# A long convolution in front of a gated MLP: cosine phases made on TensorE for twelve groups, and a fourth of the transform's copies on VectorE

## The chip, the cores and the metric

The kernel runs on one core of a Trainium2 chip. The metric is the time of one execution in microseconds (us) on the device, the median of several runs. In the profile PE is TensorE, DVE is VectorE, ACT is ScalarE, POOL is GpSimd and SP is SyncE, which issues DMAs.

## The reference

```python
# x: 2048 positions x 576 channels; 128 complex poles for each channel
dt = exp(log_dt);  logdA = dt * (A_re + 1j*A_im);  dB = dt * B
P = exp(logdA[:, :, None] * arange(2048))             # 576 x 128 x 2048
K = einsum("dn,dnl,dn->dl", C, P, dB).real            # the convolution's kernel
h = layernorm(x) * (1 + ca) + sa
x = x + ga * (causal_conv(h, K) + h * Dskip)          # through FFTs of length 4096
h = layernorm(x) * (1 + cb) + sb
z = gelu(h @ w_in)                                    # 576 -> 4608
z1, z2 = z[..., :2304], layernorm(z[..., 2304:])
x = x + gb * ((z1 * (w_sp @ z2 + b_sp)) @ w_out)      # w_sp: 2048 x 2048
```

`sa` to `gb` are six rows of `silu(c) @ w_mod`.

## The kernel before

**Two parts.** `ssm` is the convolution; the class `Mlp` is the rest. The change lies in `ssm`, in about the first 155 us. There every operation is issued in the order in which the program writes it (the wrapper at lines 223 and 224 pins it, which is why the profile gives line 224 for nearly everything). That order is a written table, `ORDER` (from line 55): each word is one step of a unit, such as `t5` for the next step of `t_unit(5)`, and `Steps.go` runs them one by one. Each engine takes its own instructions in this order, and an instruction that waits holds all behind it on its engine.

**Poles.** `poles` computes the logarithms and angles of the poles, first for chunk 0 (steps `O0`), then for chunks 1 to 3 (steps `P0`); each number is split into three bfloat16 parts (`pt`) and stored to DRAM (`pa_d`, `pb_d`). `poles_load` (line 392) reads a chunk back into `lb`, `lc` and `la`: two halves at partitions 0 to 47 and 64 to 111. The partitions 32 to 63 of `lb` are first set to zero by POOL, since one matmul reads all 112.

**Groups.** There are 36 groups `g` of 16 channels. `e_unit` makes the magnitudes: matmuls of `lb` with the table `sel` into a double PSUM bank, then exponentials on ACT into `et`. `t_unit` (line 578) makes the phases. For a group in `ROUNDED` (among them all of 0 to 13) PE fills one `ps` tile of 128x1024 with twelve matmuls: it adds a large constant, adds the phase in turns (`phases` with `lc` and `la`), takes the constant away again, so that only the rounded number of turns is left, and subtracts the phase. What stands in PSUM is then minus the phase's fraction of a turn. I call these twelve matmuls a fill. DVE writes its absolute value to half of an `ft` tile (for the cosine); ACT writes the sine to the other half, straight from PSUM, and then the cosine from the absolute value, as a sine with a bias of a quarter turn. The `ps` tiles are two (`ps2`, shared with `e_unit`), the `ft` tiles three, the single-bank `pk` tiles four (`ps1`); the table `PLAN` says which use takes which. `p_unit` (line 621) multiplies `ft` with `et` on DVE, `kg_unit` contracts the products over the poles on PE and `k1_unit` makes the first transform stage of the kernel.

**The input's transform.** `mod_unit` makes the rows of `silu(c) @ w_mod`: matmuls of `wm`, `k_a` or `k_b` with `ec`, a copy to `mpart` on ACT, a second matmul with ones, then `gar`, `cga` and `sga`. `ln_rows` scales rows of x with `cga` on DVE. `ln_half` (line 540, sixteen calls, steps `A0` to `A15`) transforms them: matmuls into four `pk` tiles, four copies of 128x288 from there to `st1o` on ACT, and a DMA issued by POOL. `st1o` has two buffers.

After that, groups, the products with the input's transform and the way back (`u_unit`, `z_unit`, `v_unit`, `y_unit`) go on until about 340 us, followed by the MLP.

Of the kernel before, what the change touches and what calls it, by code (L numbers as in the profile page):

```python
# [9 lines left out]
F32 = mybir.dt.float32  # L10
# [20 lines left out]
COPIED = set()  # L31
PLAN = {
    "et": "0123401232013423014021304123024104120",
    "ft": "012021201201021201202102101201012102",
# [7 lines left out]
    "ps": "01010010100101111010101001010101010101011001001110100101001011000101010101010101010101010101010101010101010101"  # L42
        "0101",
# [11 lines left out]
B0 O0 O0 O0 O0 B2 O0 O0 O0 O0 B7 O0 B1 O0 O0 O0 B6 O0 O0 O0 O0 O0 O0 x0 O0 O0 O0 O0 P0 S0 O0 S0 B3 O0 O0 i2 O0 O0 O0 P0 M2 O0 O0 S0 S0 B4 P0 S0 O0 Q0 P0 e1 S0 M2 e1 i1 e0  # L55
P0 P0 g0 e1 e0 P0 e0 e1 P0 t1 t2 i0 g1 O0 M2 e0 P0 M1 t1 t2 t1 P0 P0 t0 w3 P0 M1 t0 M2 t1 t0 t2 M1 M0 M1 M0 t0 e2 j1 R1 P0 p1 M3 t2 M0 p1 M3 R0 e2 R3 e6 p1 M0 B5 e2 M0 e6
M3 w4 k1 e4 e2 P0 M3 k1 O0 P0 e3 11 p0 e4 11 e6 M4 M0 e5 p0 P0 p0 e6 S1 S1 p2 M4 k0 M4 p2 11 R2 p2 e5 k0 e5 S1 M0 M3 M0 P0 k2 M4 e5 M0 P0 t5 k2 A0 e3 A0 S1 A0 A0 A0 w5 t5
S1 e3 P0 e3 A0 t3 S1 A1 t5 A1 A1 r2 A1 P0 t3 R4 A1 t7 A0 R5 A1 A2 A2 O0 P0 t3 t3 A2 A2 t4 P0 A1 A2 A2 A3 p3 A2 A3 t5 P0 r3 A3 A3 t4 t4 j2 M4 10 10 e4 A3 A3 A3 e4 12 p3 12
e7 p3 e7 P0 e7 R7 t7 10 R6 P0 p5 S2 12 k3 e8 e7 O0 k3 e8 A4 S2 A4 S2 A4 e8 S2 A4 A4 A4 e8 p5 P0 A5 t4 A5 A5 P0 A5 p5 A5 p4 A5 t7 a4 A4 A5 t6 A6 A6 A6 p4 A6 t6 A6 p4 A6 t8
A7 A7 P0 t7 A7 A7 O0 k4 A6 P0 S2 A7 13 t6 p7 A7 k4 t8 p7 R9 14 13 O0 k5 P0 P0 a5 t6 14 14 t8 p7 Q1 13 t8 M5 x3 k7 P0 e11 R8 A7 k5 M5 S3 k7 S3 A8 A8 e11 R11 e9 A8 e10 e11  # L60
P0 e9 e11 P0 p6 S3 S3 A8 P0 A8 R10 t10 A8 e10 A9 t10 A9 A9 A9 p8 p8 r6 e10 A9 A9 t9 e10 t10 A10 A8 P0 A10 A10 A10 A9 t11 p6 A10 A10 17 P0 t10 M5 p6 17 k6 M5 p8 t11 t9 17
k6 A11 A11 r7 S3 t11 t11 e12 A11 A11 Q2 15 R13 A11 A11 A10 p11 k8 t9 15 15 R12 A11 k8 A12 p11 A12 e12 A12 p11 A12 e14 A12 t14 A12 A13 e14 p10 A13 t14 A13 R15 e9 p10 A13
p10 A13 R14 A13 e9 t14 A12 e12 t12 e12 A14 A14 t9 A14 t15 A14 A14 t12 A13 t14 A14 t12 A15 A15 t14 O0 O0 A15 e16 k10 P0 A15 P0 A15 16 A15 P0 O0 p9 t12 k11 16 M5 p9 A14 A15
p9 C0 16 t14 18 c1 k10 f0 18 110 k11 18 110 e14 U2 110 U1 U0 t15 p12 111 t15 111 z2 111 t15 u2 t16 p12 u2 U5 p12 u0 e14 k9 c0 z2 z2 u0 k9 t16 k12 U4 p14 u1 19 U14 t16 U7
e16 k12 e15 19 t16 19 U23 e13 e15 e15 e16 u1 e15 c3 u7 e16 e13 p14 u4 u7 e13 u4 p14 c2 p15 z1 z1 e13 t13 U29 v2 u14 U6 t16 v2 p15 z4 U10 u14 t13 u6 t13 p15 t18 k15 z4 u6
u5 t16 k15 z1 p16 t18 p16 u29 e18 u5 U15 v1 z0 t13 u29 t18 e17 X1 t18 v1 U3 e18 115 115 u10 v1 v2 z0 u10 z0 X3 p16 e17 115 k14 k14 u3 b1 e17 e22 u3 p13 U12 e22 t17 e17
# [20 lines left out]
def consts():  # L87
# [64 lines left out]
    sel = np.zeros((112, 2368))  # L152
    sel[:48, :1024] = sel[64:, :1024] = half
# [7 lines left out]
    sel[:48, 1024:1280] = sel[64:, 1280:1536] = rge.reshape(48, 256)  # L161
# [75 lines left out]
def ssm(tc, I, x1_d, consts_s, dram, mod_d, mlp):  # L237
# [6 lines left out]
    with ExitStack() as ctx:  # L244
# [23 lines left out]
        sel = tb.tile([112, 2368], BF, name="sel", bufs=1)  # L268
# [132 lines left out]
        def rows(c0, w):  # L401
            return [sel[64 * h:64 * h + 48, c0:c0 + w] for h in range(2)]

        def halves(t, gi):
            return [t[64 * h:64 * h + 48, gi] for h in range(2)]
# [134 lines left out]
        def ln_half(k):  # L540
# [22 lines left out]
        def e_unit(g):  # L563
# [10 lines left out]
            T.matmul(pb, lb[:, gi], sel[:, 1024:1536], start=True, stop=True)  # L574
# [3 lines left out]
        def t_unit(g):  # L578
            c, gi = divmod(g, 9)
            pa = ps2()  # L580

            def phases(cols, start, stop):
                for k, (n, c0) in enumerate(zip(("lc", "la"), cols)):
                    for h, (l, r) in enumerate(zip(halves(lt[n, c], gi), rows(c0, 256))):
                        T.matmul(pa[:, h].rearrange("p (c k j) -> p k c j", c=8, k=2)[:, k], l, r, start=start, stop=stop, skip_group_check=True)

            def magics(c0, start):
                for h, (l, r) in enumerate(zip(rows(c0, 128), rows(2048, 64))):
                    T.matmul(pa[:, h].rearrange("p (c j) -> p c j", c=8), l, r[:, None, :].to_broadcast([48, 8, 64]), start=start, stop=False,
                             skip_group_check=True)  # L590
# [1877 lines left out]
```

## Time and profile before

| | |
|---|---|
| runs | 1691.24 to 1698.08 us, median 1694.87 of 3 |
| profiled execution | 1691.0 us, its span 1688.9 us |
| PE, DVE, ACT busy over the span | 96%, 77%, 52% |
| of the 20 us from 60 to 80: PE, DVE, ACT busy | 13.3, 19.3, 19.7 |
| from 80 to 100 | 16.3, 19.4, 18.3, granted clock 0.67 |
| from 120 to 140 | 15.4, 19.6, 19.4, granted clock 0.98 |
| from 220 to 240 | 20.0, 20.0, 19.6, granted clock 1.00 |

PE's busy time is modelled from pipelined matmuls, so a busy PE is not PE at its peak. The granted clock is the share of TensorE's full clock. In the rows of the timeline the columns are the start in us, the duration in us, the engine, the operation as output<-inputs, its shape, and in brackets the idle time of the engine just before it and what ended it. An engine begins an instruction before the one ahead has quite ended, so the step from start to start is shorter than the duration.

### The profile page before, as it was taken

Reading aid. Unit: us, or ns where it says so; the run is one execution under the profiler, and the core shown is the slowest. Engines: PE = TensorE matmul, PEld = TensorE weight load, DVE = VectorE, ACT = ScalarE, POOL = GpSimd, SP = SyncE. Lnnn points to the kernel's source line nnn. Section 1 sums busy time; section 2 is a strip of 40 time slices with the busy share of each in tenths; the row PEclk is TensorE's granted clock in tenths of the full one; section 3 lists DMA queues with packets and bytes.
Section 4 is the critical chain, followed back from the end, with each engine's and each line's share of the span. In section 5 each row is a group of like instructions: output and inputs, shape, how many; then the busy total and the mean of one; then the engine's idle time right before and its main releaser. Section 6 shows DMA issues by size and latency. Waiting matters only on the chain.

```text
span 1688.9 us, 39922 instructions
## 1 busy us (share of the span) xinstructions
PE 1615.6 (96%) x16868; PEld 1235.7 (73%) x16868; DVE 1298.4 (77%) x2241; ACT 873.8 (52%) x1307; POOL 209.7 (12%) x340
## 2 busy tenths in 40 slices
PE   3778999989999999999999999999999999999999
PEld 1344677755555557778878888888888888888887
DVE  7898999867989877988997776894443487787555
ACT  6889999675776664555444433342321133353221
POOL 3251111112222110000000000000111100111100
PEclk9978999999999999999999999999999999999999
DMA  9667645596888898776738887664667573777560
GB/s 231 170 215 229 203 140 176 171 317 208 280 287 243 251 261 297 242 270 234 249 118 302 282 292 257 219 218 166 232 213 243 189 221 121 275 281 252 189 241 29
DMA packets 186402, 380.61 MB, mean 225 GB/s; under 512 B 38464, under 2 KB 105792, under 8 KB 185456
## 3 DMA queue, kind: packets, MB, share of 16 engines
q1 hardware_dynamic: 145216, 182.10, 35.2%
q0 software_dynamic: 34528, 169.11, 30.1%
q10 hardware_dynamic: 6480, 26.86, 3.9%
q8 instruction: 132, 2.16, 0.5%
q14 instruction: 46, 0.38, 0.1%
HBM read 272.73 MB, written 105.29 MB: 224 GB/s over the span
## 4 chain that ended last, share of the span: by engine, by line
PE 77%; DVE 7%; DMA 3%; issue 2%; ACT 2%; SPq 0%; POOL 0%; ACTq 0%; DVEq 0%; POOLq 0%
PE ps L224 58%; PE pz L224 10%; PE pk_b L224 2%; PE pk_a L224 2%; DMA zset<-set_d 2%; PE pk_c L224 2%; PE pk_d L224 1%; DVE zset L224 1%; DVE gt L224 1%; DVE bsz L224 1%; PE ps_a L224 0%; PE ps_b L224 0%; DMA v_d<-v_a 0%; PE pt L224 0%; DMA uu_a<-in_x 0%
## 5 line engine op out<-in xcount | busy, mean ns | idle before, releaser
L224 PEld LDWEIGHTS <-zset 128*128 128x128 f16 x7182 | 702.2, 98 | 86.5 <-DMA zset<-set_d 2.0
L224 PE MATMUL ps<-wsp,zset 128*128 128x256 f16 x6048 | 666.8, 273 | 2.2 <-DMA zset<-set_d 1.1
L224 PE MATMUL pz<-wz,nt 128*128 128x512 f16 (+1 forms) x1120 | 220.8, 358 | 1.5 <-ACT nt L224 1.0
L224 ACT ACTIVATE z<-gt 128x1024 f16<-128x1024 f32 x56 | 59.0, 1054 | 250.4 <-DVE gt L224 250.4
L224 PEld LDWEIGHTS <-nt 128*128 128x128 f16 x1120 | 109.4, 98 | 107.1 <-ACT nt L224 1.5
L2164 POOL DMA_DIRECT2D zset<-set_d x96 | 50.8, 529 | 862.5 <-PE ps L224 619.7
L224 PE MATMUL ps<-wout,z 128*128 128x288 f16 x1092 | 138.4, 286 | 0.0
L224 DVE SCALAR_TENSOR_TENSOR gt<-ps,sc,bsp 128x512 f32<-128x512 f32 x36 | 27.0, 749 | 143.0 <-PE ps L224 141.3
L224 PEld LDWEIGHTS <-z 128*128 128x128 f16 x1176 | 115.1, 98 | 28.9
L224 DVE TENSOR_TENSOR raw<-raw 128x256 f32<-128x256 f32 (+3 forms) x238 | 126.8, 539 | 7.7 <-DMA raw<-z_d 3.5
L224 PE MATMUL ps<-n2o,zset 128*128 128x256 f16 x1134 | 128.2, 273 | 0.0
L224 DVE SCALAR_TENSOR_TENSOR gt<-ps,sc,gt 128x512 f32<-128x512 f32 (+1 forms) x180 | 122.2, 696 | 7.6
L224 ACT ACTIVATE zset<-raw 128x1792 f16<-128x1792 f32 x48 | 81.1, 1691 | 59.3 <-PE ps L224 21.6
L224 DVE TENSOR_TENSOR zset<-raw,zset 128x1792 f16<-128x1792 f32 x48 | 96.9, 2020 | 15.7 <-ACT zset L224 15.7
L224 DVE TENSOR_TENSOR z<-ps,z 128x512 f32<-128x512 f32 (+1 forms) x126 | 72.0, 599 | 32.3 <-ACT z L224 25.9
L224 ACT ACTIVATE z<-pz,sc 128x512 f32<-128x512 f32 (+1 forms) x96 | 51.9, 574 | 39.9 <-PE pz L224 32.7
L224 ACT ACTIVATE wsp<-raw,sc 128x1792 f16<-128x1792 f32 x25 | 44.5, 1783 | 46.2 <-DVE raw L224 40.2
L224 ACT ACTIVATE z<-z,sc 128x1024 f32<-128x1024 f32 x21 | 24.1, 1148 | 76.0 <-DVE z L224 72.3
L224 ACT ACTIVATE z1b<-gt 128x512 f16<-128x512 f32 (+1 forms) x22 | 17.7, 821 | 84.0 <-DVE gt L224 84.0
L224 PE MATMUL ps<-n2q,wf 128*128 128x512 f16 x252 | 55.7, 379 | 0.0
L224 DVE BATCH_NORM_STATS2 bsz<-z 128x6 f32<-128x384 f32 x96 | 48.4, 548 | 5.0 <-ACT z L224 4.4
L224 DVE SCALAR_TENSOR_TENSOR wsp<-raw,sc,wsp 128x1792 f16<-128x1792 f32 x25 | 52.0, 2078 | 0.3 <-ACT wsp L224 0.3
(793 smaller groups left out, 2772.0 us busy)
## 6 DMA issues: line engine op xcount, KB each, us to landing
zset<-set_d POOLq DMA_DIRECT2D x96, 896.0 KB, 5.2
raw<-z_d SPq DMA_DIRECT2D x48, 512.0 KB, 5.6
set_d<-zset ACTq DMA_DIRECT2D x24, 896.0 KB, 6.4
z_d<-z POOLq DMA_DIRECT2D x32, 576.0 KB, 8.2
zset<-wa_d POOLq DMA_DIRECT2D x18, 896.0 KB, 4.9
raw<-in_w_spT SPq DMA_DIRECT2D x25, 512.0 KB, 4.4
set_d<-zset SPq DMA_DIRECT2D x12, 896.0 KB, 5.8
wst<-in_w_in SPq DMA_DIRECT2D x8, 1024.0 KB, 9.3
```

The lines of the kernel that those rows point to most:

```text
L224: return self.tc.keep_in_program_order(f(*a, **k))
L2164: self.nc.gpsimd.dma_start(o, self.set_d[f, j - 1] if j else self.wa_d[f])
```

## The change

For the groups 0 to 11 (`TWICE`) PE makes a second fill into the other `ps` tile, a quarter turn on: `sel` has one more row for each half, which holds a quarter, and the partition behind each half of `lc` and `la` is set to one, so that the matmuls of `phases` take 49 rows instead of 48. Both sine and cosine are then a plain sine on ACT, straight from PSUM; the absolute value on DVE falls away. The steps of such a unit are still four. `lb`, `lc` and `la` become two fixed tiles each, and their constant parts are set once by DVE: the first tiles in `begin(0)`, the second in `begin(4)`; POOL's four memsets go. In `ln_half` the third of the four copies goes from ACT to DVE (`SHARED`). `ORDER` and the rings `ft` and `ps` of `PLAN` are written anew for the early part, up to the last `A` steps.

```diff
+TWICE = set(range(0, 12))
+SHARED = {2}
...
-P0 P0 g0 e1 e0 P0 e0 e1 P0 t1 t2 i0 g1 O0 M2 e0 P0 M1 t1 t2 t1 P0 P0 t0 w3 P0 M1 t0 M2 t1 t0 t2 M1 M0 M1 M0 t0 e2 j1 R1 P0 p1 M3 t2 M0 p1 M3 R0 e2 R3 e6 p1 M0 B5 e2 M0 e6
+e0 P0 P0 g0 e1 e0 P0 e0 e1 P0 t1 t1 i0 g1 O0 M2 e0 P0 M1 t1 P0 P0 w3 P0 M1 M2 t0 t1 t0 t0 t2 t0 t2 M1 M0 M1 M0 t2 e2 j1 R1 P0 t2 p1 M3 M0 p1 M3 R0 e2 R3 e6 p1 M0 B5 e2
...
-    sel = np.zeros((112, 2368))
+    sel = np.zeros((113, 2368))
...
+        sel[h + 48, :256] = sel[h + 48, 768:1024] = 0.25
+        sel[h + 48, 1536:2048] = -0.25
...
+        ltiles = {n: [tb.tile([112 if n == "lb" else 113, 9, 128], BF, name=n + i, bufs=1) for i in "ab"] for n in ("lb", "lc", "la")}
+
+        def fill(i):
+            for n, t in ltiles.items():
+                if n == "lb":
+                    V.memset(t[i][32:64], 0.0)
+                else:
+                    V.memset(t[i][32:64], 1.0)
+                    V.memset(t[i][96:113], 1.0)
...
-                t_ = tb.tile([112, 9, 128], BF, name=n)
-                if n == "lb":
-                    Q.memset(t_[32:64], 0.0)
+                t_ = ltiles[n][c % 2]
...
             for g, pm in enumerate(pms):
-                A.activation(o[:, g], pm[:, :HC], AF.Copy)
+                if g in SHARED:
+                    V.tensor_copy(o[:, g], pm[:, :HC])
+                else:
+                    A.activation(o[:, g], pm[:, :HC], AF.Copy)
...
+            def rounded(pa, r):
+                magics(pa, 2112, True)
+                phases(pa, (768, 0), False, False, r)
+                magics(pa, 2240, False)
+                phases(pa, (1536, 1792), False, True, r)
...
+            if g in TWICE:
+                rounded(pa, 48)
+                yield
+                pc = ps2()
+                rounded(pc, 49)
+                yield
+                ct, f = places()
+                A.activation(f, pa, AF.Sin, scale=-TWO_PI)
+                yield
+                A.activation(ct, pc, AF.Sin, scale=-TWO_PI)
+                return
...
             if n == 0:
+                fill(0)
                 p0 = poles(0, 1, G, ring(tb, [128, 1536], F32, "et", 5))
...
             elif n == 4:
+                fill(1)
                 S.dma_start(small, I["c_small"].rearrange("p (i c) -> p i c", i=7))
```

`places` takes the `ft` tile, as `t_unit` did before. `magics` and `phases` do what they did, with the tile and the number of rows as arguments. In the two rows of `ORDER`, between the first `M1` steps (the matmuls of `k_a`) and the third (the matmul with ones that `cga` waits for), there stand the PE steps of `t0` once before; now both PE steps of `t0` and both of `t2`, with ACT's steps of `t1` and `t0` among them.

On DVE, in the pole work for chunks 1 to 3, after layer norm's means (`nm`), the change puts the second set of memsets:

```order
58 L228 TENSOR_SCALAR nm<-nm 128x4
59 L228 MEMSET lbb 32x576
60 L228 MEMSET lcb 32x1152
61 L228 MEMSET lcb 17x1152
62 L228 MEMSET lab 32x1152
63 L228 MEMSET lab 17x1152
64 L228 TENSOR_SCALAR t_rnd<-t_n_A_im 128x432
```

Before, `nm` and `t_rnd` followed each other. A little further on, DVE before the change has the absolute values of the first three groups around the splitting of the poles (`t_tau` to `t_sq`), ahead of `cga`:

```order
80 L224 TENSOR_TENSOR t_n_B_im<-t_n_B_im,t_rnd 128x432
81 L224 TENSOR_SCALAR ft_a<-ps_a 128x1024
82 L224 TENSOR_SCALAR ft_b<-ps_b 128x1024
83 L224 TENSOR_SCALAR t_tau_223<-t_n_A_im 128x432
84 L224 TENSOR_SCALAR t_rnd<-t_tau_223 128x432
85 L224 TENSOR_TENSOR t_tau_223<-t_tau_223,t_rnd 128x432
86 L224 TENSOR_TENSOR t_sq_403<-t_n_A_re,pt 128x432
87 L224 TENSOR_TENSOR t_sq_405<-t_n_A_im,pt 128x432
88 L224 TENSOR_SCALAR ft_c<-ps_a 128x1024
89 L224 SCALAR_TENSOR_TENSOR cga<-pk_c,gar 128x288
```

In the change the rows 81, 82 and 88 are gone and the others stand in the same order. On ACT, at the same place, before the change:

```order
40 L224 ACTIVATE mpart<-pk_d 128x288
41 L224 ACTIVATE gar<-pk_a 128x288
42 L224 ACTIVATE gar<-pk_b 128x288
43 L224 ACTIVATE ft_a<-ft_a,consts_s 128x1024
44 L224 ACTIVATE ft_c<-ps_a 128x1024
45 L224 ACTIVATE ft_b<-ps_b 128x1024
46 L224 ACTIVATE mpart<-pk_a 128x288
47 L224 ACTIVATE mpart<-pk_b 128x288
48 L224 ACTIVATE ft_c<-ft_c,consts_s 128x1024
```

and in the change (`ft_a` is group 1 in both; group 0 is `ft_c` before and `ft_b` now, group 2 `ft_b` before and `ft_c` now):

```order
40 L228 ACTIVATE mpart<-pk_d 128x288
41 L228 ACTIVATE gar<-pk_a 128x288
42 L228 ACTIVATE gar<-pk_b 128x288
43 L228 ACTIVATE ft_a<-ps_b 128x1024
44 L228 ACTIVATE ft_b<-ps_a 128x1024
45 L228 ACTIVATE ft_b<-ps_b 128x1024
46 L228 ACTIVATE mpart<-pk_a 128x288
47 L228 ACTIVATE mpart<-pk_b 128x288
48 L228 ACTIVATE ft_c<-ps_a 128x1024
```

The cosines now read a `ps` tile, and both sines of group 0 stand ahead of `mpart<-pk_a`.

More of the change, by code (lines that the diff above doesn't have):

```diff
@@ L41 @@
         "021320312031230123012310312031203120312031320120312031203123013021300101010101010101010101010101010101010101",
-    "ps": "01010010100101111010101001010101010101011001001110100101001011000101010101010101010101010101010101010101010101"
-        "0101",
+    "ps": "01010101010100101010101010101010101010101011010101011001001110100101001011000101010101010101010101010101010101"
+        "0101010101010101",
     "st1o": "010101010101010101",
@@ new lines @@
+p4 A6 t6 A6 t8 p4 A6 A7 A7 P0 t6 A7 t8 A7 O0 k4 A6 P0 S2 A7 13 p7 A7 k4 p7 R9 14 13 O0 k5 P0 P0 a5 t8 14 14 p7 Q1 t8 13 M5 x3 k7 P0 e11 R8 A7 k5 M5 S3 k7 S3 A8 A8 e11
+R11 e9 A8 e10 e11 P0 e9 e11 P0 p6 S3 S3 A8 P0 A8 R10 t10 A8 e10 A9 t10 A9 A9 A9 p8 p8 r6 e10 A9 A9 e10 t10 A10 A8 P0 A10 t11 A10 A10 A9 t10 t11 p6 A10 A10 17 P0 M5 p6
+t11 t9 17 k6 M5 p8 17 k6 t11 A11 A11 t9 r7 S3 A11 A11 t9 e12 Q2 15 R13 A11 A11 t9 A10 p11 k8 15 15 R12 A11 k8 A12 p11 A12 e12 A12 p11 A12 e14 A12 t14 A12 A13 e14 p10
@@ L84 @@
+v24 z34 L4 y5 v34 z35 L9 v34 y5 y8 L3 z25 z30 y5 L7 v35 z25 z25 u32 v35 u32 v25 z30 v25 L10 X19 L13 X11 v30 v26 L0 X17 X12 v25 z32 v30 L11 L20 v30 z33 z32 v32 X9 z33
+v32 v33 v33 v34 W9 L12 L6 L1 v32 L14 v33 X13 y11 X10 X16 W13 y11 v35 y9 y13 W12 W10 W14 y12 L15 W16 y10 y13 L8 W17 L18 y12 y11 X14 W15 X15 W18 y9 y9 W19 y10 L19 y16 y16
+y17 L22 y14 X18 y17 y15 y19 y18 y14 y12 y10 y15 y19 L16 y15 L17 y18 y16 y13 y17 y19 y14 y18
 """
@@ L151, in consts @@
     half = np.concatenate([rgt.reshape(48, 256), rpe.reshape(48, 512), rpt.reshape(48, 256)], axis=1)
-    sel = np.zeros((112, 2368))
-    sel[:48, :1024] = sel[64:, :1024] = half
+    sel = np.zeros((113, 2368))
+    sel[:48, :1024] = sel[64:112, :1024] = half
     for h in range(0, 112, 64):
@@ L160, in consts @@
         sel[rows, 2240:] = -1.0
-    sel[:48, 1024:1280] = sel[64:, 1280:1536] = rge.reshape(48, 256)
+    sel[:48, 1024:1280] = sel[64:112, 1280:1536] = rge.reshape(48, 256)
     ones = np.zeros((128, 128))
@@ L267, in ssm @@
         tb = tabs.enter_context(tc.tile_pool(name="tb", reuse_waits="tile", bufs=2))
-        sel = tb.tile([112, 2368], BF, name="sel", bufs=1)
+        sel = tb.tile([113, 2368], BF, name="sel", bufs=1)
         dsk = tb.tile([128, 144], F32, name="dsk", bufs=1)
@@ L399, in poles_load, with rows, halves @@
                 lt[n, c] = t_
[L401 to L405, printed above, removed]
+        def rows(c0, w, k=48):
+            return [sel[64 * h:64 * h + k, c0:c0 + w] for h in range(2)]
+        def halves(t, gi, k=48):
+            return [t[64 * h:64 * h + k, gi] for h in range(2)]
         ec = cp.tile([96, 6], F32, name="ec")
@@ L573, in e_unit @@
             pb = ps1()
-            T.matmul(pb, lb[:, gi], sel[:, 1024:1536], start=True, stop=True)
+            T.matmul(pb, lb[:, gi], sel[:112, 1024:1536], start=True, stop=True)
             yield
@@ L579, in t_unit, with phases @@
             c, gi = divmod(g, 9)
-            pa = ps2()
[L582 to L590, printed above, removed]
+            def phases(pa, cols, start, stop, r=48):
+                for k, (n, c0) in enumerate(zip(("lc", "la"), cols)):
+                    for h, (x, y) in enumerate(zip(halves(lt[n, c], gi, r), rows(c0, 256, r))):
+                        T.matmul(pa[:, h].rearrange("p (c k j) -> p k c j", c=8, k=2)[:, k], x, y, start=start, stop=stop, skip_group_check=True)
@@ new lines, in magics @@
+            def magics(pa, c0, start):
+                for h, (x, y) in enumerate(zip(rows(c0, 128), rows(2048, 64))):
+                    T.matmul(pa[:, h].rearrange("p (c j) -> p c j", c=8), x, y[:, None, :].to_broadcast([48, 8, 64]), start=start, stop=False,
+                             skip_group_check=True)
+            def rounded(pa, r):
[3 more added lines that the diff above has]
+                phases(pa, (1536, 1792), False, True, r)
@@ new lines, in places @@
+            def places():
+                cs = tt[g] = ring(tb, [128, 2, 2, 512], F32, "ft", 3)
+                return cs[:, 0], cs[:, 1]
+            pa = ps2()
+            if g in TWICE:
[9 more added lines that the diff above has]
+                return
@@ L592, in t_unit @@
             if g in ROUNDED:
-                magics(2112, True)
-                phases((768, 0), False, False)
-                magics(2240, False)
-                phases((1536, 1792), False, True)
+                rounded(pa, 48)
                 yield
-                cs = tt[g] = ring(tb, [128, 2, 2, 512], F32, "ft", 3)
-                ct, f = cs[:, 0], cs[:, 1]
+                ct, f = places()
                 if g in ON_ACT:
@@ L606, in t_unit @@
             else:
-                phases((768, 0), True, True)
+                phases(pa, (768, 0), True, True)
                 yield
-                cs = tt[g] = ring(tb, [128, 2, 2, 512], F32, "ft", 3)
-                ct, f = cs[:, 0], cs[:, 1]
+                ct, f = places()
                 A.activation(f, pa, AF.Copy, bias=MAGIC)
```

52 lines of the change are left out of this document (23 added, 29 removed).

## The prediction, made before the change was run

> **What bounds the kernel now.** I read the page first, then the chain that ended last, then the busy times by stretch, then the instructions in order of time around the places that the change touches. The first three:
>
> ```profile
> PE 1615.6 (96%) x16868; PEld 1235.7 (73%) x16868; DVE 1298.4 (77%) x2241; ACT 873.8 (52%) x1307; POOL 209.7 (12%) x340
> ```
> ```profile
> 158.48 1.03 ACT ft_b L224
> ...
> 343.04 7.52 DMA v_d<-v_a
> ...
> 614.31 161.42 PE ps L224 x1246
> ```
> ```profile
> 45.70:57.10 11.40, 10.55 (x78) 4.64 (x76) 8.85 (x15) 9.66 (x15) 0.00 (x0) 1.00 0.71 206
> 57.10:75.00 17.90, 13.39 (x337) 7.46 (x338) 17.62 (x29) 17.65 (x41) 7.95 (x13) 1.00 0.60 151
> 75.00:112.00 37.00, 28.33 (x567) 15.09 (x567) 33.86 (x71) 33.19 (x65) 19.54 (x30) 0.68 0.64 203
> 112.00:140.00 28.00, 20.92 (x496) 11.69 (x504) 27.49 (x55) 26.39 (x51) 10.26 (x18) 0.99 0.72 229
> 140.00:158.00 18.00, 15.23 (x386) 8.52 (x370) 13.01 (x17) 16.28 (x33) 3.46 (x5) 0.74 0.56 181
> ```
>
> The columns of the last view are stretch, its length, busy PE, weight loads, DVE, ACT, POOL, then granted clock, DMA share and GB/s. The whole span is PE's, but the change acts only before about 155 us, and there PE is the least loaded of the three: from 57 to 158 us (100.9 us) it stands idle 23.0, DVE 8.9, ACT 7.4. The chain that ended last is followed back to 158 us without a hole, so what is won before that reaches the end: what follows (the loads behind `v_d`, then the long PE run) is started by the work before it. So I ask by how much the work at 158 us comes earlier. ACT is the pacer, DVE close behind.
>
> **What goes and comes.** Twelve absolute values leave DVE; sixteen copies go from ACT to DVE; twelve sines for the cosine read PSUM instead of `ft`; twelve fills (twelve matmuls each) come to PE; ten memsets come to DVE and four leave POOL. In order of time, the steps of one engine from start to start:
>
> ```profile
> 129.12 1.22 DVE L224 TENSOR_SCALAR ft_a<-ps_a 128x1024 int32<-128x1024 int32 x1
> 130.25 1.22 DVE L224 TENSOR_SCALAR ft_b<-ps_b 128x1024 int32<-128x1024 int32 x1
> ...
> 138.29 0.41 ACT L224 ACTIVATE st1o_a<-pk_d 128x288 f32<-128x288 f32 x1
> 138.58 0.42 ACT L224 ACTIVATE st1o_a<-pk_b 128x288 f32<-128x288 f32 x1
> ```
> ```profile
> 131.07 1.02 ACT L224 ACTIVATE ft_a<-ps_a 128x1024 f32<-128x1024 f32 x1
> 131.97 1.15 ACT L224 ACTIVATE ft_a<-ft_a,consts_s 128x1024 f32<-128x1024 f32 x1
> 133.01 0.41 ACT L224 ACTIVATE st1o_b<-pk_b 128x288 f32<-128x288 f32 x1
> ...
> 56.55 0.45 DVE L224 TENSOR_TENSOR sga<-pk_a,gar 128x288 f32<-128x288 f32 x1
> 56.91 0.45 DVE L224 TENSOR_TENSOR sga<-pk_b,gar 128x288 f32<-128x288 f32 x1
> ```
>
> An absolute value holds DVE 1.13 us, a copy holds ACT 0.29, a sine from PSUM 0.90 against 1.04 for the cosine from SBUF. DVE's own copy of 128x288 out of PSUM is not in the trace; the nearest rows are the two sums from `pk` of that size, 0.36 a step, and I take that.
>
> **Stage A, the memsets.** The five before the first load stand on DVE ahead of the first pole operation; the other five stand in the middle of the pole work for chunks 1 to 3.
>
> ```profile
> L224 DVE MEMSET wso<- 64x128 uint32 x5 | 0.8, 165 | 0.4
> ```
> ```profile
> 0.88 0.06 DVE L187 MEMSET consts_s<- 128x1 f32 x1
> 3.15 0.31 DVE L224 TENSOR_TENSOR et_a<-t_dt,et_a 128x144 f32<-128x144 f32 x1 [2.22 <-DMA et_a<-in_A_A_im]
> ...
> 26.34 0.26 DVE L224 TENSOR_SCALAR ss<-ss 128x4 f32<-128x4 f32 x1 [0.63 <-ACT st1o_a L224]
> ```
> ```profile
> 17.30 0.68 ACT L224 ACTIVATE st1o_a<-ln_x 128x576 f32<-128x576 f32 x1 [0.69 <-DMA ln_x<-in_x]
> ...
> 36.02 0.56 ACT L224 ACTIVATE t_q<-t_n_B_im 128x432 f32<-128x432 f32 x1 [0.48 <-DVE t_n_B_im L224]
> ...
> 45.78 0.41 ACT L224 ACTIVATE mpart<-pk_d 128x288 f32<-128x288 f32 x1 [3.11 <-PE pk_d L224]
> ```
>
> One column takes 0.06 us and 128 take 0.165, so 0.83 ns a column: 1.01 us for 1152 columns and 0.53 for 576, together 0.53 + 4 x 1.01 = 4.6 a set, an estimate. The first set ends at 0.94 + 4.6 = 5.5 instead of 3.15, 2.3 late; ACT has 0.7 of slack at 17.30, so 1.6 arrive at the second set. That adds 4.6, less DVE's idle 0.63: `t_n_B_im` and with it ACT at 36.02 come 5.6 later. ACT's next idle time, 3.1 before `mpart<-pk_d`, absorbs 3.1: **+2.5 us**. Bounds: at a quarter of the price 1.2 a set, which is within 2.2 and 3.1 us of idle: 0. At POOL's price for the same memset (1.05 us in the row below) 5.3 a set: 3.1 late at first, less 0.7, plus 5.3, less 0.6 and 3.1: +4.0.
>
> ```profile
> 24.24 1.05 POOL L224 MEMSET lb<- 32x1152 bf16 x1
> ```
>
> The Trainium skill (VectorE: DVE Perf Modes, section Zero memsets can be issued as uint32) says that a memset takes one cycle per element whatever the type, and that only zeros are halved; that makes 0.6 + 4 x 1.2 = 5.4 us a set, an estimate, and the stage +4.2 instead of +2.5. That the four memsets leave POOL gains nothing: `la`, on which the first fills wait, is issued after a DMA and not after them.
>
> **Stage B, 45.7 to 57 us.** Before, one fill (group 0) stands between the matmuls of `k_a` and those of `mpart`; now four stand there, each waiting for ACT to empty one of the two `ps` tiles.
>
> ```profile
> 45.68 0.61 PE L224 MATMUL ps_a<-sel 48*128 48x512 bf16 x2
> ...
> 47.50 1.33 PE L224 MATMUL pk_c<-mpart,small 128*128 128x288 f32 x2
> 47.61 1.22 DVE L224 TENSOR_SCALAR ft_c<-ps_a 128x1024 int32<-128x1024 int32 x1 [4.54 <-PE ps_a L224]
> ...
> 48.93 0.46 DVE L224 SCALAR_TENSOR_TENSOR cga<-pk_c,gar 128x288 f32<-128x288 f32 x1
> ...
> 51.67 0.39 PE L224 MATMUL ps_a<-sel,lb 48*128 48x512 bf16 x2
> ```
> ```profile
> 46.67 1.16 ACT L224 ACTIVATE ft_a<-ft_a,consts_s 128x1024 f32<-128x1024 f32 x1
> ...
> 51.36 0.41 ACT L224 ACTIVATE mpart<-pk_a 128x288 f32<-128x288 f32 x1 [0.55 <-PE pk_a L224]
> ...
> 57.12 1.02 ACT L224 ACTIVATE et_d<-ps_a 128x1024 f32<-128x1024 f32 x1
> ```
> ```profile
> 169.94 0.97 PE ps_b L224 x12
> ```
>
> A fill took 1.82 us here (45.68 to 47.50, 512 columns in 0.61) and 0.97 later (512 columns in 0.39, from 51 us on). In the old times: ACT empties the first cosine tile from 46.67 to 47.6; then come the second fill of group 0 at 1.82, the first of group 2 at about 1.4 (half of it slow), the second at 0.97: 51.8, plus 0.7 for `pk_c<-mpart`, and `cga` starts at 52.5 instead of 48.93. That is **+3.6 us** for DVE, whose next work, the rows of layer norm, stands behind `cga`, and for ACT, whose `mpart<-pk_a` waits for matmuls behind it; ACT's sines on the way are 0.2 cheaper: **+3.4**. All fast: 47.6 + 2.9 + 0.7 = 51.2, +2.3; all slow: 47.6 + 5.5 + 1.4 = 54.5, +5.6. DVE's three absolute values here gain nothing, since it stood idle 4.54 us anyway.
>
> **Stage C, 57 to 158 us.** ACT loses 16 x 0.29 = 4.6 and 9 x 0.14 = 1.3: **-5.9 us**. DVE loses 9 x 1.13 = 10.2 and gets 16 x 0.36 = 5.8: -4.4. DVE would so come out 1.5 later than ACT, but it has a wait that takes this up (who waited for whom from 57 to 158 us; total, times, longest):
>
> ```profile
> DVE pg_b L224 <- PE pk_c L224: 4.5, 1, 4.5
> ...
> ACT kab_a L224 <- PE pk_b L224: 1.0, 1, 1.0
> ```
>
> The nine fills put 9 x 0.97 = 8.7 us (9 x 1.82 = 16.4 at the slow clock) into PE's 23.0 idle; that cover holds unless the clock stays low. Behind each new copy on DVE's queue stand products that PE waits for, and a `pk` tile is free only when DVE gets to it; I take nothing for that, with +-1. Of ACT's 7.4 idle, waits on PE and on DVE's absolute values among them, I take back a fifth, -1.5, bounds 0 and -7.4. ACT_TABLE_LOADs stay thirty.
>
> **Sum.** 2.5 + 3.4 - 5.9 - 1.5 = -1.5 us on a span of 1688.9 (execution 1691.0, 2.1 around it; the median of the runs, 1694.87, lies 3.9 above). Applied to the median: 1693.4 us. From 0.5%, 8.5 us, on, a measurement of this kernel can tell it from no change.
>
> **Rivals.**
> (1) PE warms and the covers hold: the memsets hide (A 0), the fills run fast (B 2.3 - 0.2), ACT saves 5.9 and gets all its idle 7.4 back: -11.2, 1683.7, faster. For it: the low clock, 0.68 from 75 to 112 and 0.74 from 140 to 158, stands where PE idles most, and PE gets more to do there. Against: ACT's idle is partly DMA. It decides if the granted clock of 75 to 112 rises to about 1. The Trainium skill (TensorE: Matmul & The Clock Gate, Part 1) says that the clock is throttled by default and that a window of sustained work releases it; the trace agrees in that the fills fall from 1.82 to 0.97 us after some 5 us of work from 45.7 on, and does not in that it stays at 0.68 from 75 to 112 us with PE 77% busy. Chance 0.10.
> (2) PE becomes the bound from 75 to 112 us, slower: about six of the nine fills fall there, at 1.82 us 10.9, against 8.7 idle of which the order makes perhaps half usable: +6.6, and the savings of this stretch, half of C's 5.9, are hidden. A and B stay: 2.5 + 3.4 + 6.6 - 3.0 = +9.5, 1704.4. For it: ready tiles wait for `ps`, of which there are two, now filled twice per group. It decides where the clock stays at 0.68 and more than 4 us of idle can't be used. Chance 0.08.
> (3) The forecast, chance 0.82: ends between -7.3 (A 0, B +2.1, C -5.9, idle -3.5) and +7.1 (A +4.0, B +5.4, of C -2.3 left). Both stay within 0.5%.
>
> Range: the ends of (3) on the median are 1687.6 and 1702.0; the lower is moved half way to rival (1), which needs no new cost to come true, so 1685 to 1702.
>
> **What would show it.** Right: a set of five memsets near 4.6 us, `cga` at about 55 instead of 48.9, DVE's absolute values gone with ACT busy over 0.95 from 60 to 140, the first long `ps` run of the MLP starting within 5 us of 614.3. Wrong: `mpart<-pk_d` not later than 45.8 (A falls), `cga` before 51 (B falls), PE over 0.95 busy from 75 to 112 at a low clock (rival 2), granted clock 1 there with ACT's idle gone (rival 1), or a change after 158 us that the start of that run doesn't explain.

## The result and the profile after

The changed kernel took 1743.91 us (median of 4 runs, 1740.23 to 1750.84); the kernel before, run beside it, 1696.47. The ratio is 1.0288, 95% interval 1.0247 to 1.033: about 49 us slower by the ratio, 47 by the two medians. The prediction was 1693.4 us, 1685 to 1702, with a chance of 0.08 for slower.

All of it is lost ahead of the MLP. The page of the changed kernel, the busy times and one row of the chain that ended last:

```profile
PE 1639.2 (94%) x17012; PEld 1251.8 (72%) x17012; DVE 1301.4 (74%) x2255; ACT 869.9 (50%) x1291; POOL 205.4 (12%) x336
```
```profile
675.23 161.42 PE ps L228 x1246
```

The long run of PE that stood at 614.31 stands at 675.23, 60.9 us later, and takes the same 161.42 us. The profiled executions lie 59.8 apart (1691.0 and 1750.84, each at an end of its kernel's runs).

About half of the 60.9 is there before the first exponential. SP issues the table `sel` and then `small`; PE's first matmul with `sel` and ACT's exponential behind it follow. Before the change, rows of the timeline:

```profile
9.17 0.43 SPq L224 DMA_DIRECT2D sel<-in_c_sel  x1
9.64 0.44 SPq L224 DMA_DIRECT2D small<-in_c_small  x1
...
30.74 1.02 ACT L224 ACTIVATE et_b<-ps_a 128x1024 f32<-128x1024 f32 x1
```

The same rows after the change:

```profile
9.34 0.33 SPq L228 DMA_DIRECT2D sel<-in_c_sel  x1
9.83 12.07 SPq L228 DMA_DIRECT2D small<-in_c_small  x1
...
58.00 0.61 PE L228 MATMUL ps_a<-sel,lba 48*128 48x512 bf16 x2 [21.32 <-DMA sel<-in_c_sel]
58.65 1.02 ACT L228 ACTIVATE et_b<-ps_a 128x1024 f32<-128x1024 f32 x1 [21.51 <-PE ps_a L228]
```

PE waits 21.32 us for a load that was issued at the same time as before and has one row more. SP's next issue takes 12.07 us instead of 0.44. The DMA view from 0 to 70 us says how long the two loads took, before the change and after it (the last column is us from issue to landing; `sel` has none after the change):

```profile
sel<-in_c_sel SPq DMA_DIRECT2D x1, 518.0 KB, 10.0
small<-in_c_small SPq DMA_DIRECT2D x1, 448.0 KB, 11.0
```
```profile
sel<-in_c_sel SPq DMA_DIRECT2D x1, 522.6 KB
small<-in_c_small SPq DMA_DIRECT2D x1, 448.0 KB, 51.3
```

The matmul that waited for it starts 48.7 us after the issue: 522.6 KB (of 1024 bytes) in that time is 11 GB/s, where 518.0 KB in 10.0 us was 53. And from 58 us on, when `sel` has landed and the loads issued behind it are still under way, a stretch of the changed kernel reads like this (columns as in the prediction, the last two the DMA share and GB/s):

```profile
58.00:64.00 6.00, 6.00 (x31) 2.38 (x31) 0.00 (x0) 5.29 (x8) 0.00 (x0) 1.00 0.06 26
```

A share of 0.06, a sixteenth, fits a single busy engine, which then moves 26 GB/s; that it had its part of every other load to move until then, and so gave `sel` only 11, is argued and not shown. The Trainium skill (DMA: Bandwidth & Descriptors, section Why a DMA increments its semaphore by 16 and not by 1) says that a transfer runs on the largest number of engines up to sixteen that divides the size of the outermost dimension on both of its sides, so that 112 rows use sixteen and 113, a prime, one. The trace agrees, with its share of 0.06.

The rest of the loss comes later. `cga`, which the forecast had at 55, stands at 78.52 (48.93 before), 29.6 late; so 31.3 more are lost from there to the MLP. ACT, forecast to be busier than 0.95 from 60 to 140, is busy 61.9 of these 80 us, 0.77. The same work lies about 60 us later, so I set 60 to 160 before against 118 to 218 after:

```profile
60.00:160.00 100.00, 77.17 (x1711) 42.24 (x1711) 91.04 (x167) 92.62 (x186) 39.37 (x62) 0.83 0.64 198
```
```profile
118.00:218.00 100.00, 75.12 (x1628) 44.50 (x1627) 69.18 (x131) 67.48 (x124) 29.56 (x47) 0.81 0.55 173
```

DVE and ACT, which paced this part, are busy 69 and 67 of 100 us instead of 91 and 93; the absolute values and copies that went, 10.2 and 4.6 us by the prediction's count, are the smaller part of that. PE is not busier than before, and the granted clock is nearly the same, 0.81 against 0.83. No engine is the bound there: the engines wait for one another.

### The profile page after: what moved, and what is told of

Read it like the earlier page. It is cut to its first block, busy times and chain, and to the rows that moved or that the text cites. A ratio compares the mean times of both kernels' runs of the same rounds, so it can differ in the third digit from the quotient of the medians.

```text
span 1749.1 us, 40202 instructions
## 1 busy us (share of the span) xinstructions
PE 1639.2 (94%) x17012; PEld 1251.8 (72%) x17012; DVE 1301.4 (74%) x2255; ACT 869.9 (50%) x1291; POOL 205.4 (12%) x336
## 4 chain that ended last, share of the span: by engine, by line
PE 81%; DVE 4%; ACT 4%; issue 3%; DMA 2%; SPq 0%; POOL 0%; ACTq 0%; DVEq 0%; POOLq 0%
PE ps L228 57%; PE pz L228 12%; PE pk_a L228 3%; PE pk_b L228 2%; PE pk_c L228 2%; PE pk_d L228 2%; DVE zset L228 1%; PE ps_a L228 1%; PE ps_b L228 1%; DVE gt L228 1%; DMA zset<-set_d 1%; PE pt L228 1%; ACT L228 1%; DMA v_d<-v_a 1%; DMA u_d<-st1o_b 0%
```

## The experiments

Times are medians; each ratio is against the kernel before, run beside it, and 0.001 of it is 1.7 us. "Place" and "slot" below are these: `ORDER` differs from the one before only in where the steps of `t0` to `t11` stand (and `e12`, by two places), and a group with a second fill holds both `ps` tiles from its second step to its third. From the memsets on, every run that starts from the changed kernel has the load of `sel` split in two.

### The load

First the load of 113 rows, undone in the changed kernel, and done alone in the kernel before.

```diff
-                S.dma_start(sel, I["c_sel"])
+                S.dma_start(sel[:112], I["c_sel"][:112])
+                S.dma_start(sel[112:], I["c_sel"][112:])
```

> The changed kernel, with the table sel loaded in two transfers: its first 112 rows, then row 112 alone. Theory 'load' (all of the loss comes from the one transfer of 113 rows, which took some 49 us for 523 KB where the one of 112 rows landed 10 us after its issue): the first exponential, ACT et_b, is back near 31 to 41 us instead of 58.65, the MLP's long run on ps starts between 605 and 625 us instead of 675.2, and the time is 1685 to 1703 us, the forecast's own sum. Rival 'fills' (the second fills and the new order of the work cost it: TensorE or the PSUM slots bind): 1735 to 1750 us, as the changed kernel. Rival 'memsets' (the ten memsets ahead of the poles start everything late): also 1735 to 1750 us.

Measured: 1724.39 us, ratio 1.0181 (1.0156 to 1.0205). The exponential is back at 31.5, but only some 18 us of the 49 are. So the theory "load" is true for its place and false as the whole cause.

```diff
-    sel = np.zeros((112, 2368))
+    sel = np.zeros((113, 2368))
...
-        sel = tb.tile([112, 2368], BF, name="sel", bufs=1)
+        sel = tb.tile([113, 2368], BF, name="sel", bufs=1)
```

> The kernel before, with one row of zeros put under the table sel, so that its load has 113 rows; nothing else differs and the row is not read. Theory 'load': slower than the kernel before by 40 to 60 us, 1735 to 1755 us, with sel landing near 58 us and SP's next load held for about 12 us at its issue. Rivals 'fills' and 'memsets': no difference, 1688 to 1700 us.

Measured: 1720.81 us, ratio 1.0161 (1.0136 to 1.0186): one row of zeros that nothing reads costs the kernel before 27 us. Rows of its timeline:

```profile
9.24 0.34 SPq L224 DMA_DIRECT2D sel<-in_c_sel  x1
9.77 17.12 SPq L224 DMA_DIRECT2D small<-in_c_small  x1
...
62.03 0.61 PE L224 MATMUL ps_a<-sel,lb 48*128 48x512 bf16 x2 [28.89 <-DMA sel<-in_c_sel]
```

The place is as expected, the price lower: the matmul starts 31.9 us late (30.09 before), and 27 of them reach the end. Then two other numbers of rows, 116 under the kernel before and 128 under the changed one:

> The kernel before, with four rows of zeros under sel: 116 = 4 x 29 rows in one transfer. If the rows of a transfer are dealt over as many DMA engines as divide their number and 16 (four here, one for 113, sixteen for 112), it lands about a quarter of 49 us after its issue, 12 to 16 us, so near 22 to 26 us, ahead of its first reader at 30 us, and the time is that of the kernel before within 8 us. If every number of rows that is no multiple of 16 falls to one engine: landing near 58 us and 1735 to 1755 us.

> The changed kernel, with sel padded with zeros to 128 rows in one transfer. Theory 'load' by the divisor: sixteen engines again, the load lands 10 to 12 us after its issue, and the time is that of the split load within 5 us, 1685 to 1703. If the bytes or the rows above 112 counted: as late as with 113 rows or later, 1735 us or more. Rivals 'fills' and 'memsets': 1735 to 1750.

The DMA view of the two, 116 rows first:

```profile
sel<-in_c_sel SPq DMA_DIRECT2D x1, 536.5 KB
small<-in_c_small SPq DMA_DIRECT2D x1, 448.0 KB, 19.2
```
```profile
sel<-in_c_sel SPq DMA_DIRECT2D x1, 592.0 KB, 7.6
small<-in_c_small SPq DMA_DIRECT2D x1, 448.0 KB, 8.1
```

116 rows: 1698.88 us in one run, within 8 us of the kernel before; no matmul waits for `sel`, and `small` behind it lands in 19.2 us, between 11.0 and 51.3. Its own landing is not in the trace. 128 rows: 1725.24, ratio 1.0186 (1.0156 to 1.0216), the same as the split, with 13% more bytes than 113 rows and a landing after 7.6 us. So it is not the size, and the four numbers of rows fit the rule of the divisors; that 116 uses just four engines no row shows.

### The memsets

With the load mended, 31 us are left. Rows of the split kernel's ACT, where DVE's second set of memsets ends at 30.9:

```profile
39.86 0.56 ACT L228 ACTIVATE t_lw<-t_n_B_re 128x432 f32<-128x432 f32 x1 [4.11 <-DVE t_n_B_re L228]
43.39 0.56 ACT L228 ACTIVATE t_q<-t_n_B_im 128x432 f32<-128x432 f32 x1 [2.97 <-DVE t_n_B_im L228]
...
47.81 1.02 ACT L228 ACTIVATE ft_a<-ps_a 128x1024 f32<-128x1024 f32 x1
...
49.93 0.41 ACT L228 ACTIVATE mpart<-pk_d 128x288 f32<-128x288 f32 x1
```
```profile
57.87 0.46 DVE L228 SCALAR_TENSOR_TENSOR cga<-pk_c,gar 128x288 f32<-128x288 f32 x1 [7.42 <-PE pk_c L228]
```

The second of ACT's rows stood at 36.02 before (a row of the prediction), the third, the first Sin pass, at 40.44, and `mpart<-pk_d` at 45.78; DVE's `cga` stood at 48.93. I moved both sets to GpSimd, at the start of the program.

```diff
-                    V.memset(t[i][32:64], 0.0)
+                    G.memset(t[i][32:64], 0.0)
...
                 fill(0)
+                fill(1)
```

> The changed kernel with the split load, and the ten memsets of both sets issued by GpSimd at the program's start, where it is idle until 13 us, in place of VectorE's. With the split load alone 31 us of the loss are left (1724 us): 8.5 of them are there at the store of the second pole parts (66.6 us where the kernel before has 58.2), the other 23 come between 67 and 190 us. Theory 'memsets' (VectorE's second set of memsets, 5.6 us from 25.3 us on, holds the second chunk's pole operations, on which ScalarE waits at 35 to 43 us in front of the Sin passes that free the PSUM slots): cga is back from 57.9 to 50 to 54 us and the time falls by 5 to 9 us, to 1715 to 1719. If the four fills themselves make stage B late (forecast's stage B, or a slot that waits for a Sin): cga at 56 to 58 us and 1721 to 1727.

Measured: 1718.13 us, ratio 1.0125 (1.0101 to 1.0149), some 9 us less than the split; `cga` at 53.53 instead of 57.87. The next two runs go together. Both have all copies on ScalarE, as before the change; the second of them also has cheap memsets on GpSimd, over half as many elements of four bytes (a float whose bits are two bfloat16 ones), the second set at 39 us behind a load.

```diff
-SHARED = {2}
+SHARED = set()
```

> The changed kernel with the split load and with all four copies of a ln_half on ScalarE again (SHARED empty); second fills, order and memsets stay. Theory 'copy' (VectorE takes its work in order, so the third copy, which waits for TensorE's products in pk, holds the products and LayerNorm work behind it: VectorE waits 18 us for pk and ft in front of st1o copies between 66 and 180 us, and ScalarE and TensorE then wait for VectorE): the time falls from 1724 by 8 to 14 us, to 1710 to 1716. Theory 'order': as the split load, 1719 to 1727. Theory 'ScalarE' (that the copies taken from ScalarE saved time): slower by 3 to 8 us, 1727 to 1732.

```diff
-                    V.memset(t[i][32:64], 1.0)
+                    G.memset(t[i][32:64].bitcast(F32), ONES)
...
             q.dma_start(x4s[i], I["x"][:, 4 * i:4 * i + 4])
+            if i == 1:
+                fill(1)
```

> The changed kernel with the split load, all copies on ScalarE, and the memsets on GpSimd over half as many four-byte elements: the first set at the start, the second behind the load of ln_x at 40 us, where GpSimd is idle until 58. Second fills and order stay. Theories 'memsets' and 'copy' together: 6 to 8 us less than without shared copies alone, about 1703 to 1709, with the second pole parts stored at 61 to 63 us in place of 66.6. What is then left above the kernel before (some 10 to 15 us) is TensorE's second fills with the order made for them. Theory 'order' without 'copy': 1714 to 1720.

Measured: 1726.07 (1.0202, 1.018 to 1.0225) without the shared copies, 1720.2 (1.0162, 1.0143 to 1.0182) with cheap memsets as well. So the memsets on DVE cost 7 to 9 us, and theory "copy" falls: the shared copies do not hold anything up. With cheap memsets the two rows from above stand earlier than in the kernel before:

```profile
42.47 0.41 ACT L229 ACTIVATE mpart<-pk_d 128x288 f32<-128x288 f32 x1 [0.69 <-PE pk_d L229]
```
```profile
48.46 0.46 DVE L229 SCALAR_TENSOR_TENSOR cga<-pk_c,gar 128x288 f32<-128x288 f32 x1 [6.26 <-PE pk_c L229]
```

Done alone in the kernel before the shared copies change nothing either:

> The kernel before with the third copy of each ln_half on VectorE, and nothing else. Theory 'copy': slower than the kernel before by 8 to 14 us, 1702 to 1708. Theory 'order': within 4 us of the kernel before.

Measured: 1693.15 us, ratio 1.0011 (0.9994 to 1.0028). Sixteen copies taken from ACT gain nothing that can be measured.

### The second fills

Three runs asked early on whether PE's work or its slots cost the rest. The first drops the second fills, with the absolute values back on DVE, and keeps the order and the rings; the second keeps two of the twelve matmuls (and so leaves out the cosine's phases); the third adds twelve matmuls a group to the kernel before and nothing else.

```diff
-                rounded(pc, 49)
...
+                V.tensor_single_scalar(ct.bitcast(I32), pa.bitcast(I32), 0x7FFFFFFF, op=ALU.bitwise_and)
```

> The changed kernel with the split load, without the second fills of groups 0 to 11: their cosine comes from VectorE's absolute value again, in the third step of the group's four; order, memsets, shared copies and tiles stay. Theory 'TensorE' (144 more matmuls of about 0.13 us each at the granted clock of 0.8, on the engine that others wait for between 67 and 190 us) and theory 'slots' (the second fill needs the other PSUM slot of ps, which waits for a Sin pass): the 23 us are gone, 1697 to 1706. Theory 'order' (the order of the work is to blame): 1715 to 1727.

> The changed kernel with the split load, where the second fill is two matmuls of zeros in place of twelve; slots, waits and ScalarE's passes stay. It leaves out the cosine's phases. Theory 'TensorE': most of the 23 us are gone, 1700 to 1710. Theory 'slots': as the split load, 1718 to 1727.

```diff
+                for _ in range(2 if g < 12 else 1):
                     magics(2112, True)
                     phases((768, 0), False, False)
                     magics(2240, False)
                     phases((1536, 1792), False, True)
```

> The kernel before, where groups 0 to 11 make their phases twice into the same slot, twelve matmuls more for each and nothing else. Theory 'TensorE': slower than the kernel before by 12 to 25 us, 1706 to 1718. Theories 'slots' and 'order': within 5 us of the kernel before.

Measured: 1718.83 (1.0138, 1.0119 to 1.0157), 1713.89 (1.0108, 1.009 to 1.0127) and 1696.57 (1.0023, 1.0006 to 1.004). The third is the surprise: 144 more matmuls cost 4 us, 0.3 a group. This is a net price, since TensorE ran faster with them: the granted clock is 0.990 in the mean of these ten runs and 0.984 in the twelve of the kernel before beside them, and in the profiled execution it is 0.87 from 60 to 160 us, against 0.83 above:

```profile
60.00:160.00 100.00, 76.52 (x1704) 45.72 (x1697) 83.88 (x157) 86.89 (x173) 36.03 (x56) 0.87 0.58 182
```

From 60 us on, 2 of the 40 timeline rows for two matmuls of 512 columns in its fills are longer than 0.5 us; in the kernel before 11 of 23 are. But ten matmuls fewer in each second fill gain 12 us (1.0181 to 1.0108) where that fill waits for a slot. PE waits as long for Sin passes in front of a fill in the split kernel as in this one (14.1 and 14.0 us from 30 to 160), so these 12 us are not fewer such waits. And the first run, without any second fill, keeps 23 us; I read this at first as a sign against slots, which was wrong: its ring still set one tile of each group's pair aside, so that groups 0 to 8 all went through `ps_a` and 9 to 11 all through `ps_b`. The next two runs mended that. Both have the kernel before's operations in the changed kernel's order; the second gives the groups the two tiles in turn.

> The operations of the kernel before (no second fill, VectorE's absolute value in the group's second step, all copies on ScalarE, only lb's two memsets, on GpSimd at the start) in the changed kernel's order, with the split load. Theory 'order': 1708 to 1718, since the order alone then carries what is left of the loss. Theories 'copy' and 'TensorE': 1690 to 1699, as the kernel before.

```diff
-    "ps": "01010101010100101010101010101010101010101011010101011001001110100101001011000101010101010101010101010101010101"
+    "ps": "010101010110101010101010101010110101010110010011010110101100110001010010010101010101010101010101010101010101010101010101",
...
-                ps2()
```

> As the run of the order alone (the operations of the kernel before in the changed kernel's order, 1717 us), but with the PSUM slots of ps given to the groups' phases in turn; there, all phases of groups 0 to 9 went into one slot, since the other was kept for second fills that were not made. Theory 'one slot' (a group that holds both slots, or a run of groups that use one of them, keeps TensorE from filling the next group's phases while ScalarE reads the last): most of the 24 us are gone, 1692 to 1701. Theory 'place' (the steps of groups 0 to 11, moved by up to 54 places of the order, stand too late in the engines' queues, whatever slot they use): 1708 to 1720.

Measured: 1717.27 (1.0147, 1.0122 to 1.0172) and 1703.4 (1.0063, 1.004 to 1.0086). The second tile alone gives back 14 us of 25; the place of the steps costs about 11, or 8 above the ground that is measured below. PE's waits for a Sin pass in front of a fill (30 to 160 us; total, times, longest), in the kernel before, with one tile and with both in turn:

```profile
PE ps_a L224 <- ACT ft_a L224: 1.5, 1, 1.5
PE ps_a L224 <- ACT ft_c L224: 1.5, 1, 1.5
```
```profile
PE ps_a L228 <- ACT ft_c L228: 5.2, 3, 2.8
PE ps_a L228 <- ACT ft_a L228: 2.4, 2, 1.8
PE ps_a L228 <- ACT ft_b L228: 2.4, 1, 2.4
PE ps_b L228 <- ACT ft_b L228: 1.8, 1, 1.8
PE ps_b L228 <- ACT ft_c L228: 0.9, 1, 0.9
```
```profile
PE ps_a L227 <- ACT ft_c L227: 1.5, 1, 1.5
```

3.0, 12.7 and 1.5 us. The same rows of the changed kernel with mended load, cheap memsets and no shared copies (1720.2 us):

```profile
PE ps_a L229 <- ACT ft_c L229: 4.6, 3, 2.3
PE ps_a L229 <- ACT ft_a L229: 1.8, 1, 1.8
PE ps_b L229 <- ACT ft_c L229: 1.7, 2, 0.9
PE ps_b L229 <- ACT ft_a L229: 1.0, 1, 1.0
PE ps_b L229 <- ACT ft_b L229: 0.8, 2, 0.6
```

9.9 us. In which groups the loss arises, three runs of that kernel told, with second fills and the new places for some groups alone, and a run of their common ground without any.

```diff
-TWICE = set(range(0, 12))
+TWICE = {0, 1, 2}
```

> Second fills for groups 0 to 2 alone, whose steps stand as in the changed kernel; all other steps stand as in the kernel before; split load, all copies on ScalarE, four-byte memsets on GpSimd. All twelve groups in this setting took 1720 us, 26 above the kernel before. Theory 'one slot': 3 to 6 us of the 26 belong here, 1695 to 1700. Theory 'TensorE' (about 0.9 us a group): 1693 to 1697.

> The same with second fills for groups 3 to 8 alone. Their first fills move back furthest in the order (group 5 by 17 places, group 7 by 54). Theory 'one slot': 10 to 17 us of the 26 belong here, 1703 to 1711. Theory 'TensorE': 1696 to 1701.

> The same with second fills for groups 9 to 11 alone. Theory 'one slot': 4 to 8 us, 1697 to 1702. Theory 'TensorE': 1693 to 1698. If groups 9 to 11 were faster than the kernel before, 1685 to 1690, a part of the change would be worth keeping.

> The ground that the three runs by groups stand on, with no second fill at all: the kernel before's order and operations, with sel's 113 rows loaded in two transfers, the fixed tiles, and the ten four-byte memsets on GpSimd. If the parts add up (9, 12 and 13 us for groups 0 to 2, 3 to 8 and 9 to 11 against 26 for all twelve), the ground itself costs (34 - 26) / 2 = 4 us: 1696 to 1700. If the ground costs nothing, 1691 to 1695, each part alone loses most of what it would lose beside the others, and second fills are a loss wherever they stand.

Measured: 1703.66 (1.0053, 1.0027 to 1.0078), 1706.6 (1.0069, 1.0047 to 1.0092), 1707.02 (1.0072, 1.0045 to 1.01), and the ground 1695.97 (1.0018, 1.0004 to 1.0032). Less the ground's 3 us the parts are 5.9, 8.6 and 9.1, together 23.7, against 24.4 for all twelve (1.0162 less 1.0018). They add up, and none is a gain: 1.4 to 3.0 us a group. Each interval is some 4 us to either side, so which groups lose most is not told. Nothing shows that the distance which a step moved in the order sets the price: group 7's first fill moved furthest, by 54 places, and groups 3 to 8 come out lowest, at 1.4 each.

Last, a second fill that takes no second tile: the kernel before's order, and the tile of the first fill made again once ACT has read it.

```diff
-TWICE = set(range(0, 12))
+TWICE = {0, 2, 3, 6, 8, 11}
...
+                A.activation(f, pa, AF.Sin, scale=-TWO_PI)
+                yield
+                rounded(pa, 49)
+                yield
+                A.activation(ct, pa, AF.Sin, scale=-TWO_PI)
```

> The same ground with second fills that need no second slot: the phases of groups 0, 2, 3, 6, 8 and 11 (those for which the order of the kernel before leaves the slot free until the group's fourth step) are made again, a quarter turn on, in the slot of their first fill once ScalarE has read it. Theory 'one slot' (what costs is that no fill runs ahead): within 4 us of the ground, and faster than the kernel before if VectorE's six absolute values (1.2 us each) counted: 1688 to 1697. Theory 'second fills lose wherever they stand' (TensorE's queue, and the cosine's Sin behind a fill of its own): 1698 to 1706.

Measured: 1710.23 us, ratio 1.0097 (1.0074 to 1.012), 13.4 above the ground for six groups, 2.2 a group. PE's waits for Sin, here and on the ground:

```profile
PE ps_a L228 <- ACT ft_a L228: 2.6, 2, 1.5
PE ps_a L228 <- ACT ft_c L228: 2.6, 2, 1.4
PE ps_b L228 <- ACT ft_c L228: 1.1, 1, 1.1
```
```profile
PE ps_a L222 <- ACT ft_a L222: 0.9, 1, 0.9
```

So second fills lose without a second tile too. Here ACT waits for them in turn, 10.4 us in five waits, where it has no such wait on the ground and 0.2 us in the changed kernel with mended load and memsets. The two longest:

```profile
ACT ft_b L228 <- PE ps_a L228: 4.4, 1, 4.4
ACT ft_c L228 <- PE ps_b L228: 2.5, 1, 2.5
```

In these runs a fill that must wait for a Sin pass thus costs 1.4 to 3.0 us, and one that waits for nothing, on a faster TensorE, 0.3 (in the profile from 60 to 160 us the clock is 0.70 in this run, against 0.80 on the ground). The fill stands in PE's queue, which is taken in order; that whatever stands behind it, products and transforms, is late for DVE and ACT fits the rows, but no run shows it alone. From 60 to 160 us, on the ground and in the changed kernel with mended load and memsets:

```profile
60.00:160.00 100.00, 80.03 (x1689) 43.06 (x1679) 89.66 (x164) 91.52 (x183) 34.02 (x54) 0.80 0.62 193
```
```profile
60.00:160.00 100.00, 77.65 (x1426) 42.68 (x1433) 69.46 (x143) 76.30 (x153) 33.03 (x54) 0.78 0.52 160
```

ACT and DVE do 15 and 20 us less in the same time; about 10 of DVE's are the absolute values that fell away. The waits of PE that are named are 9 of the 24 us (9.9 less 0.9), if all of them reach the end; how the other 15 divide between the length of a fill in a waiting chain (the run with two matmuls gained 12), the place of the steps (8 without any second fill) and the clock was not taken apart further.

## Why the prediction was wrong

**The step that failed first** is the list under "What goes and comes". It counts abs, copies, sines, fills and memsets, and leaves out that `sel`'s load grows from 112 to 113 rows, though the diff shows it. One row of 112 looked like nothing; it has no term, no bound and no rival. Alone it costs 27 us. In the changed kernel mending it gives back 18, which fits a wait that hides the memsets: without it they come to the light with their 7 to 9.

**Stage A, +2.5**, was mis-sized. A single memset was near the estimate, as rows of the changed kernel's DVE show:

```profile
25.26 0.54 DVE L228 MEMSET lbb<- 32x576 uint32 x1 [0.17 <-issue]
25.99 1.02 DVE L228 MEMSET lcb<- 32x1152 bf16 x1 [0.19 <-issue]
27.29 1.02 DVE L228 MEMSET lcb<- 17x1152 bf16 x1 [0.28 <-issue]
...
30.92 0.38 DVE L228 TENSOR_SCALAR t_rnd<-t_n_A_im 128x432 f32<-128x432 f32 x1
```

0.54 and 1.02 us against 0.53 and 1.01, but a step is 1.29, with 0.28 between two, so a set takes 5.6 and not 4.6. In the split kernel the first Sin pass is then 7.4 us late (47.81 instead of 40.44), where 5.6 were forecast. The cover held: ACT's idle of 3.1 ahead of `mpart<-pk_d` is gone, and that row is 4.2 late (49.93 instead of 45.78). So against the kernel before the term is +4.2. The runs give the memsets 7 to 9, which is more; with cheap ones `mpart<-pk_d` comes 3.3 earlier than in the kernel before (42.47), and why it does no run shows. The prediction's second estimate, 5.4 a set and +4.2 by what the Trainium skill (VectorE: DVE Perf Modes, section Zero memsets can be issued as uint32) says of a memset's price, came nearer. That is partly luck, since it has 1.2 us for a memset that took 1.02, and the gaps made up for it.

**Stage B, +3.4**, was about right. From `mpart<-pk_d` to `cga` the kernel before takes 3.15 us, the split kernel 7.94 and the one with cheap memsets 5.99, so +4.8 and +2.8. The prediction puts the fills of 1.82 us down to a slow clock; its own row from 45.70 to 57.10 has a granted clock of 1.00, so what makes two matmuls of 512 columns take 0.61 us there is not shown.

**Stage C, -7.4**, had the wrong sign. In the split kernel `cga` is 8.9 us late (57.87 instead of 48.93) and the end 31, so some 22 are lost behind it, where 7.4 were to be won. Its ACT term rests on "ACT is the pacer": taking sixteen copies off it gained nothing in the kernel before. Its cover, nine fills in PE's 23 us of idle, counted work, and as work alone the fills are cheap (4 us for twelve, on a faster TensorE). What it left out is that a fill of a group's second tile, or of the next group's first, now stands behind a Sin pass that it must wait for. The second fills with their order cost 24 us, stage B among them. Rival (2) named its sign in "two, now filled twice per group", but its condition, PE over 0.95 busy at a low clock, was not met: PE was busy 78 of 100 us in the changed kernel with mended load and memsets, 77 in the kernel before. So PE's load by itself did not decide; a fill that stands in a chain of waits did, and how its price comes about is in part open, as said above.

**The sum as it came out.** Taken off one after the other, the load is 18.1 us, the shared copies are 3.6 the other way (1.0181 against 1.0202, with intervals that overlap), the memsets 6.8, the second fills with their order 24.4, and 3.0 are left for the ground. That is 48.7, the 49 measured, as it must be for differences of neighbouring runs. None of the eighteen kernels of the experiments is faster than the kernel before, so no part of the change that is worth keeping was found.

## What to carry to other kernels

Read every number of rows in a diff that a DMA carries: the load of a tile that grew from 112 to 113 rows took 48.7 us instead of 10.0 here and held the queue behind it; splitting the odd row off or padding to 128 undid it. Idle time of an engine is no promise that it covers more work there: twelve fills that waited for nothing more cost 4 us, and twelve that waited for a tile, with the order made for them, 24. So before adding a step to an in-order queue, ask which buffer it needs and who must empty it first. And price a row of like operations by the step from start to start, as these memsets show, 1.29 us for 1.02.

## What else the runs showed

The issue of the DMA behind the one of 113 rows held SP for 12.07 us in one kernel and 17.12 in the other, where it takes 0.44. And memsets on GpSimd can hold DVE: with the first bfloat16 sets there from 0.8 to 11.6 us, two small DVE operations that took 0.23 and 0.23 us in the kernel before (at 4.04 and 6.72) took 1.07 and 1.17. The first ends at 6.20, about when GpSimd's two memsets of `laa` do, at 6.11:

```profile
5.13 1.07 DVE L228 TENSOR_SCALAR t_rnd<-et_a 128x144 f32<-128x144 f32 x1
```
```profile
3.95 2.16 POOL L228 MEMSET laa<- 32x1152 bf16 x2
6.16 1.05 POOL L228 MEMSET lbb<- 32x1152 bf16 x1
```

The Trainium skill (SBUF — State Buffer, section SBUF: two separate sides) says that DVE in a mode that uses two ports shares one pair of them with GpSimd as an exclusive lock, and that the one that comes second waits for the other's whole instruction. The run agrees in these two times, while DVE's operations on two tensors beside them took their usual 0.31; that the two run in such a mode no view shows.
